# Unused tiles of 32 to 192 bytes between the tiles of a Fourier-mixing and FFN kernel, so that TensorE's weights lie 64 bytes (mod 256) above the operand streamed meanwhile

## The chip, the cores and the metric

The kernel runs on one core of one Trainium2 chip. The metric is the device time of one execution in microseconds (us); the median of several runs is compared. Engines are named as in the profile: PE is TensorE's matmuls, PEld its weight loads, DVE is VectorE, ACT ScalarE, POOL GpSimd, SP the engine that issues most DMAs.

## What is computed

Three layers follow one another on x of shape (4, 3072, 256), all float32:

```
X  = rfft(x, axis=1)                                  # layer 1: Fourier mixing
Yr = soft(Xr @ w_r - Xi @ w_i + b_r)                  # soft(v) = sign(v) * max(|v| - 0.01, 0)
Yi = soft(Xr @ w_i + Xi @ w_r + b_i)
x  = irfft(Yr + i Yi, n=3072, axis=1)
xk = mu_k * x + (1 - mu_k) * x_prev                   # layer 2: FFN with a token shift, 256 -> 1024 -> 256
xr = mu_r * x + (1 - mu_r) * x_prev
x  = sigmoid(xr @ w_r2) * ((max(xk @ w_k, 0) ** 2) @ w_v)
h  = x @ w_in                                         # layer 3: FFN 256 -> 2048 -> 256
out = (h * clip(h + 3, 0, 6) / 6) @ w_out
```

## The kernel before, in words

Each float32 operand is split in two halves, a rounded high part and a low rest, and each product is made of three matmuls: high by high, low by high, high by low (`three`, whose matmul is L156, and `m` inside `u_s`, L698). Every matmul has a weight load of its own: the left operand (the weights, up to 128 x 128) is loaded, then the right operand (192, 256 or 512 columns) is streamed past it. The load for the next matmul is issued while the current one streams. The order of PE, ACT, DVE and POOL is the order in the program (a manual schedule); only SP's queue is placed by the framework.

The work has three stretches. In the first (0 to about 800 us of the span) the Fourier layer of four batches is woven with the first FFN. `s1` (transform along 96), `s2` (transform along 32), `mix` (the complex weights), `ia` and `ib` (the inverse transforms) make the Fourier layer; `u_r`, `u_k` and `u_v` make the first FFN. While `mid` runs, one step holds 24 matmuls of mix, 6 of ia, 12 of s2 and 24 of 512 columns of the FFN. In the second (about 800 to 1105 us) the rest of the first FFN runs while DVE and ACT decode the float64 weights `wi` and `wo` of the second, and the first tile of the second FFN starts (`u_i`). In the third (about 1105 us to the end) 23 tiles of 512 tokens times 8 units, 184 units, are worked off: `u_s` (L682) makes 21 matmuls of a unit with seven products in place of eight, `u_o` (L755) the 24 that sum into the output; they are issued as 12 of u_s, 8 of u_o, 6 of u_s, 8 of u_o, 3 of u_s, 8 of u_o. All 45 stream 256 columns.

Memory: a tile pool lays its tiles one after another in SBUF, in the order in which their tags are first asked for. `cst`, `kb` and `kw` (later `sp` in the place of `kw`) stand one upon another from below, `fp` (later `w2` and `w3`) hangs from the top, so that its first tile moves down when it grows. fp takes 96,768 bytes of a partition, and 3,008 bytes lie free between kw and fp. All tiles that TensorE reads are multiples of 256 bytes in size or cut at such multiples, f1 and fi (384 bytes to each half) excepted; so the address modulo 256 is the same for all buffers of a tag and for all slices that are used.

The functions that the change touches: `stage1` (first buffers of `kb`), `load_chunks` (tag a), `load_t` (tag t), `mix` (tag y), and the body, where the pools' constants and weights are made.

Of the kernel before, what the change touches and what calls it, by code (L numbers as in the profile page):

```python
# [9 lines left out]
F32 = mybir.dt.float32  # L10
# [13 lines left out]
TOK = 512  # L24
# [79 lines left out]
def fourier_mix_ffn_kernel(  # L104
# [32 lines left out]
    cst = ctx.enter_context(tc.tile_pool(name="cst", bufs=1))  # L137
    kb = ctx.enter_context(tc.tile_pool(name="kb", bufs=1))
    kw = ctx.enter_context(ExitStack())
    kw_p = kw.enter_context(tc.tile_pool(name="kw", bufs=1))  # L140

    def ptile(name):
        return ps.tile([128, 1024], F32, tag="h", name=name)

# [5 lines left out]
    def three(o, pairs, first=True, last=True, **kw):  # L150

        n = 3 * len(pairs)
        i = 0
        for (lh, ll), (rh, rl) in pairs:
            for a, c in ((lh, rh), (ll, rh), (lh, rl)):
                nc.tensor.matmul(o, a, c, start=first and i == 0, stop=last and i == n - 1, **kw)  # L156
                i += 1
# [54 lines left out]
    def decoder(jobs, stage):  # L212

        running = []
        for n in range(2 * len(jobs) + 4):
# [5 lines left out]
                running.append(w.decode(w.load(stage, *job), *job))  # L221
            yield

    def stage1():
        w = kb.tile([128, 1024], U32, tag="gh", bufs=3, name="stw")
        return w, kb.tile([128, 2, TOK], F32, tag="gl", bufs=3, name="stt")

    with tc.manual_schedule(engines=order):
        ff = ctx.enter_context(ExitStack())
        fp = ff.enter_context(tc.tile_pool(name="fp", bufs=1, side="right"))  # L230

        f1 = cst.tile([N1, 2, N1], F32R, name="f1")
        fi = cst.tile([N1, 2, N1], F32R, name="fi")
        zero = cst.tile([128, 2, 1], F32, name="zero")
        mus = cst.tile([128, 2, 2], F32, name="mus")
        omu = cst.tile([128, 2, 2], F32, name="omu")
        half = cst.tile([128, 1], F32, name="half")
        top = cst.tile([128, 2, 1], F32, name="top")
        bias = fp.tile([128, 3, D], F32, name="bias")
        tex = fp.tile([128, 2, 64], F32R, name="tex")  # L240

# [5 lines left out]
        head = {"load": 0, "split": 0, "use": 0}  # L247
        live = {}

        def load_chunks(upto):  # L250
            while head["load"] < min(len(chunks), upto) and chunks[head["load"]][1] in ready:
                n = head["load"]
                src, _, p = chunks[n]
                a = fp.tile([128, 2, D], F32, tag="a", bufs=5, name="a")
                nc.sync.dma_start(out=a[:p], in_=src)
                live[n] = (a[:p], p)
                head["load"] += 1
# [45 lines left out]
        def load_t(b, j):  # L303

            if j >= NP + 2:
                b, j = b + 1, j - NP - 2
            if b < B:
                t = fp.tile([128, 2, 640], F32R, tag="t", bufs=3, name="tt")
                c = slice(0 if j < NP else 384, 640 if j >= 2 else 384)
                nc.gpsimd.dma_start(out=t[:, :, c], in_=tab[j, :, :, c])  # L310
                tt[b, j] = t

        def mid(b):
            gb = sc_b[b].rearrange("(j g c) n d -> j (c n) g d", g=2, c=4)
            xx, yy = {}, {}


            at = lambda j, g, dt: (512 * g + (192 if g else 256) * dt) if j == 0 else 384 * g + 192 * dt

            def s2(j):  # L320
                ((h, l),) = take(1)
                t = tt[b, j]
                p = ptile("s2")
                for g in range(2):
                    for dt in range(2):
                        d = slice(128 * dt, 128 * dt + 128)
                        hl = (h[:, g, d], l[:, g, d])
                        if j or g:
                            c = 512 * g + 192 * dt
                            three(p[:, c : c + 192], [(hl, (t[:, g, 0:192], t[:, g, 192:384]))])  # L330
                        else:
                            c = 256 * dt
                            three(p[:, c : c + 64], [(hl, (t[:, g, 0:64], t[:, g, 192:256]))])
                            three(p[:, c + 64 : c + 128], [(hl, (tex[:, 0], tex[:, 1]))])
                            three(p[:, c + 128 : c + 256], [(hl, (t[:, g, 64:192], t[:, g, 256:384]))])
                xh = fp.tile([128, 896], F32R, tag="Xh", bufs=2, name="Xh")
                xl = fp.tile([128, 896], F32R, tag="Xl", bufs=2, name="Xl")
                if j == 0:
                    split(p[:, 0:896], xh, xl)
                else:  # L340
                    two = lambda v: v.rearrange("p (g f) -> p g f", g=2)
                    split(two(p)[:, :, 0:384], two(xh[:, 0:768]), two(xl[:, 0:768]))
                xx[j] = (xh, xl)

            def mix(j):
                xh, xl = xx.pop(j)
                p = ptile("mix")
                for g in range(2):
                    pairs = []
                    for dt in range(2):  # L350
                        c = at(j, g, dt)
                        for c, w in ((c + (64 if j or g else 128), aw[0]), (c, aw[1])):
                            c = slice(c, c + 128)
                            pairs.append(((xh[:, c], xl[:, c]), (w.hi[:, dt], w.lo[:, dt])))
                    three(p[:, 256 * g : 256 * g + 256], pairs)
                y = fp.tile([128, 512], F32, tag="y", bufs=2, name="yf")
                m = fp.tile([128, 512], F32, tag="co", bufs=2, name="ym")
                yh = fp.tile([128, 512], F32R, tag="yh", bufs=2, name="yh")
                yl = fp.tile([128, 512], F32R, tag="yl", bufs=2, name="yl")
                bs = bias[:, 0:2] if j == 0 else bias[:, 1:3]  # L360
                nc.vector.tensor_add(y, p[:, 0:512], bs.rearrange("p g d -> p (g d)"))
                nc.vector.tensor_scalar(m, y, LAM, 0.0, op0=ALU.add, op1=ALU.min)
                nc.vector.scalar_tensor_tensor(y, y, LAM, m, op0=ALU.subtract, op1=ALU.max)
                yy[j] = (y, yh, yl)

            def split_y(j):
                y, *yy[j] = yy[j]
                split(y, *yy[j])

            def ia(j):  # L370
                yh, yl = yy.pop(j)
                t = tt.pop((b, j + 2))[:, :, 384:640]
                p = ptile("ia")
                for g in range(2):
                    c = slice(256 * g, 256 * g + 256)
                    three(p[:, c], [((t[:, g, 0:128], t[:, g, 128:256]), (yh[:, c], yl[:, c]))])
                sb = fp.tile([128, 4, D], F32, tag="ev", bufs=3, name="iasb")
                nc.scalar.activation(sb[:, 0:2].rearrange("p g d -> p (g d)"), p[:, 0:512], AF.Copy)
                nc.sync.dma_start(out=gb[j], in_=sb[:, 0:2])

            for j in range(NP + 1):
                if j < NP:
                    s2(j)
                load_t(b, j + 2)
                if j >= 2:
                    split_y(j - 2)
                if j < NP:
                    yield
                if j:
                    mix(j - 1)  # L390
                    fetch()
                    yield
                if 2 <= j < NP:
                    ia(j - 2)

            def end(j):
                if j + 1 < NP:
                    split_y(j + 1)
                else:
                    load_t(b, NP + 3)  # L400
                    ready.add(("b", b))
                ia(j)

            ends.extend([lambda: end(NP - 2), lambda: end(NP - 1)])
# [53 lines left out]
            later.append(plan("ib", b, 0, 8))  # L458

        aw = [Weights(fp, w, 2, D, f"aw{i}") for i, w in enumerate((w_r, w_i))]  # L460
        wr = Weights(kw_p, w_rr, 2, D, "wr")
        wk = Weights(kw_p, w_k, 2, FF1, "wk")
        wv = Weights(kw_p, w_v, 8, D, "wv")

        nc.gpsimd.dma_start(out=f1.rearrange("p s n -> p (s n)"), in_=small[:, 0 : 2 * N1])
# [348 lines left out]
        for step, _ in enumerate(stream(first)):  # L814
# [4 lines left out]
            if step in SPLIT_MIX:  # L819
                w, staged, job = plain.pop(0)  # L820
# [101 lines left out]
        for n, (i, j) in enumerate(units):  # L922
            if i == 0:
# [9 lines left out]
                if j == 3:  # L933
                    decode_to(len(wi.jobs + wo.jobs) * 2 + 4)
                    stage.close()
                    sp = ctx.enter_context(tc.tile_pool(name="sp", bufs=1))
                    sw = [sp.tile([128, 4, 8, 128], F32R, name=f"sw{c}") for c in range(2)]
                    c0, c1, c2, c3 = (sums(sp, c) for c in range(4))
                    x1 = split_s(sp, 1)
                    beside = {3: c0[:2], 4: c0[2:] + c1[:1], 5: c1[1:], 6: x1[:2], 7: x1[2:] + c2[:1]}  # L940
                    aside = c2[1:] + c3
# [44 lines left out]
```

## Time and profile before

| what | value |
|---|---|
| median of 3 runs | 2080.52 us (2079.47 to 2082.42) |
| profiled execution: its own time | 2082.47 us |
| its span, first to last instruction | 2080.7 us |
| mean granted TensorE clock, share of full speed | 0.976 |
| PE busy, matmuls | 96%, 13,928 |
| DVE, ACT, POOL busy | 74%, 64%, 2% |
| HBM read and written | 110.35 MB, 63.31 MB |

Durations of single matmuls in the profile overlap, since matmuls are pipelined; what one costs is read from the distance of one start to the next. The granted clock of 1.00 is TensorE's level of 2.4 GHz.

### The profile page before, as it was taken

How to read it: one execution, taken by the hardware profiler on the slowest of the kernel's cores; microseconds unless marked ns; L12 is line 12 of the kernel's file. 1: busy time of each engine (PE TensorE's matmuls, PEld its weight loads, DVE VectorE, ACT ScalarE, POOL GpSimd, SP SyncE). 2: the span in 40 equal slices, each digit the busy share in tenths (PEclk: the TensorE clock that was granted, in tenths of full speed). 3: DMA queues.
4: the chain of work that ended last, by engine and by line, in shares of the span. 5: the costliest groups of instructions: out<-in, count | busy, mean ns of one | idle time of the engine just before them, and what ended most of it. 6: DMA issues, size and time to landing. Idle time of an engine off the chain costs nothing.

```text
span 2080.7 us, 33798 instructions
## 1 busy us (share of the span) xinstructions
PE 1992.8 (96%) x13928; PEld 1844.5 (89%) x13928; DVE 1549.8 (74%) x1975; ACT 1323.2 (64%) x1917; POOL 35.0 (2%) x63
## 2 busy tenths in 40 slices
PE   6878999999999999889998999999999999999998
PEld 4867998898789888667787999999999999999998
DVE  3868667777677686767777777877787778777875
ACT  5556447555754565555646777777777777667775
POOL 0000000000000000000000000000000000000000
PEclk7978999999999999999999999999999999999999
DMA  9765447543653352122100001100110011001100
GB/s 265 240 205 165 123 114 228 163 142 115 216 170 111 95 179 65 63 75 77 51 31 24 29 23 29 32 21 23 30 32 21 22 31 32 21 22 31 32 11 21
DMA packets 106988, 175.85 MB, mean 85 GB/s; under 512 B 12945, under 2 KB 63314, under 8 KB 106834
## 3 DMA queue, kind: packets, MB, share of 16 engines
q1 hardware_dynamic: 96034, 141.76, 22.1%
q0 software_dynamic: 10480, 31.67, 5.7%
q8 instruction: 109, 1.79, 0.4%
q14 instruction: 45, 0.37, 0.1%
q10 hardware_dynamic: 320, 0.26, 0.0%
HBM read 110.35 MB, written 63.31 MB: 83 GB/s over the span
## 4 chain that ended last, share of the span: by engine, by line
PE 76%; DVE 14%; ACT 6%; issue 2%; DMA 2%; SPq 0%; ACTq 0%; DVEq 0%
PE oacc L776 24%; PE rq L776 15%; PE acc L156 8%; PE pk L156 7%; PE cc L776 6%; PE mix L156 5%; PE s L156 4%; DVE g L552 2%; DVE gl L553 2%; PE pr L156 2%; DVE xf L511 1%; PE ia L156 1%; DVE kl L518 1%; PE ib L421 1%; PE ib L420 1%
## 5 line engine op out<-in xcount | busy, mean ns | idle before, releaser
L776 PE MATMUL oacc<-wo_hi,gl 128*128 128x256 f32 x1536 | 426.7, 278 | 0.6 <-DVE gl L750 0.6
L776 PE MATMUL oacc<-wo_hi,gh 128*128 128x256 f32 x1536 | 427.1, 278 | 0.0
L776 PE MATMUL oacc<-wo_lo,gh 128*128 128x256 f32 x1536 | 425.4, 277 | 0.0
L776 PEld LDWEIGHTS oacc<-wo_hi,gl 128*128 128x128 f32 x1536 | 288.7, 188 | 1.0 <-DVE gl L750 0.8
L776 PEld LDWEIGHTS oacc<-wo_hi,gh 128*128 128x128 f32 x1536 | 288.5, 188 | 0.2
L776 PEld LDWEIGHTS oacc<-wo_lo,gh 128*128 128x128 f32 x1536 | 288.7, 188 | 0.0
L732 DVE TENSOR_TENSOR c<-rq,s 128x512 f32<-128x512 f32 x184 | 127.3, 692 | 184.2 <-ACT s L728 184.2
L745 DVE SCALAR_TENSOR_TENSOR g<-g,c 128x1024 f32<-128x1024 f32 x184 | 225.5, 1226 | 27.1 <-ACT g L744 17.4
L749 ACT ACTIVATE gh<-g 128x1024 fp32r<-128x1024 f32 x184 | 195.2, 1061 | 55.8 <-DVE g L745 55.8
L750 DVE TENSOR_TENSOR gl<-g,gh 128x1024 fp32r<-128x1024 f32 x184 | 223.7, 1216 | 1.2 <-ACT gh L749 1.2
L776 PE MATMUL rq<-th,sw 128*128 128x256 f32 x1104 | 217.4, 277 | 7.3 <-DVE g L606 7.3
L744 ACT ACTIVATE g<-c,half 128x1024 f32<-128x1024 f32 x184 | 211.5, 1150 | 4.1 <-DVE c L733 1.4
L712 ACT ACTIVATE s<-rq 128x512 f32<-128x512 f32 x184 | 109.9, 598 | 112.0 <-PE rq L776 111.5
L776 PEld LDWEIGHTS rq<-th,sw 128*128 128x128 f32 x1104 | 166.4, 188 | 7.5 <-DVE g L606 7.5
L156 PE MATMUL acc<-gl,wv_hi 128*128 128x512 f32 x384 | 153.8, 400 | 13.3 <-DVE gl L553 13.3
L547 ACT ACTIVATE g<-pk 128x1024 f32<-128x1024 f32 x96 | 97.6, 1016 | 106.5 <-PE pk L156 106.4
L156 PE MATMUL pk<-kh,wk_hi 128*128 128x512 f32 x384 | 152.8, 398 | 9.3 <-ACT kh L517 5.2
L776 PE MATMUL rq<-tl,sw 128*128 128x256 f32 x552 | 153.9, 279 | 2.8 <-DVE tl L679 2.8
L148 DVE TENSOR_TENSOR al<-a,ah 96x512 fp32r<-96x512 f32 (+1 forms) x176 | 114.9, 684 | 55.2 <-ACT ah L147 55.2
L156 PE MATMUL acc<-gh,wv_hi 128*128 128x512 f32 x384 | 153.2, 399 | 1.6 <-ACT gh L551 1.5
L156 PE MATMUL acc<-gh,wv_lo 128*128 128x512 f32 x384 | 152.2, 396 | 0.0
L156 PE MATMUL pk<-kl,wk_hi 128*128 128x512 f32 x384 | 151.9, 396 | 0.0
(150 smaller groups left out, 4953.0 us busy)
## 6 DMA issues: line engine op xcount, KB each, us to landing
tt<-in_tab_dram POOLq DMA_DIRECT2D x40, 640.0 KB, 4.9
yt<-sc_y SPq DMA_DIRECT2D x23, 608.0 KB, 3.9
a<-in_x_dram SPq DMA_DIRECT2D x64, 192.0 KB, 3.5
sc_a<-s1sb SPq DMA_DIRECT2D x32, 384.0 KB, 3.9
a<-sc_a SPq DMA_DIRECT2D x48, 256.0 KB, 3.2
sc_b<-iasb SPq DMA_DIRECT2D x48, 256.0 KB, 4.8
a<-sc_b SPq DMA_DIRECT2D x64, 192.0 KB, 3.1
sc_y<-ysb SPq DMA_DIRECT2D x32, 384.0 KB, 2.9
```

The lines of the kernel that those rows point to most:

```text
L148: nc.vector.tensor_sub(l, src, h.bitcast(F32))
L156: nc.tensor.matmul(o, a, c, start=first and i == 0, stop=last and i == n - 1, **kw)
L547: nc.scalar.activation(g, p, AF.Relu)
L552: nc.vector.tensor_mul(g, g, g)
L553: nc.vector.tensor_sub(l, g, h.bitcast(F32))
L712: nc.scalar.activation(s[:, 1:3].rearrange("p a n -> p (a n)"), rq, AF.Copy)
L732: nc.vector.tensor_add(c[:, 1::2], two(rq), s[:, 0:2])
L744: nc.scalar.activation(g, c, AF.Relu, bias=half, scale=1.0 / 6.0)
L745: nc.vector.scalar_tensor_tensor(g, g, 1.0, c, op0=ALU.min, op1=ALU.mult)
L749: lambda: nc.scalar.activation(h, g, AF.Copy),
L750: lambda: nc.vector.tensor_sub(l, g, h.bitcast(F32)),
L776: return lambda: nc.tensor.matmul(o, lhs, rhs, start=start, stop=stop, skip_group_check=True)
```

## The change

It adds a helper `pad` that takes an unused tile of so many bytes per partition out of a pool, and calls it at 11 places (the arrays `pad_a`, `pad_t`, `pad_y` and `padded` make those in functions happen once). No instruction reads or writes these tiles. Nothing else differs.

```diff
--- before.py
+++ after.py
@@ -139,6 +139,13 @@
     kw = ctx.enter_context(ExitStack())
     kw_p = kw.enter_context(tc.tile_pool(name="kw", bufs=1))
 
+    pads = []
+
+    def pad(pool, n):
+
+        pads.append(n)
+        pool.tile([128, n // 4], F32, name=f"pad{len(pads)}")
+
     def ptile(name):
         return ps.tile([128, 1024], F32, tag="h", name=name)
 
@@ -221,21 +228,29 @@
                 running.append(w.decode(w.load(stage, *job), *job))
             yield
 
+    padded = []
+
     def stage1():
         w = kb.tile([128, 1024], U32, tag="gh", bufs=3, name="stw")
-        return w, kb.tile([128, 2, TOK], F32, tag="gl", bufs=3, name="stt")
+        t = kb.tile([128, 2, TOK], F32, tag="gl", bufs=3, name="stt")
+        if not padded:
+            padded.append(pad(kb, 128))
+        return w, t
 
     with tc.manual_schedule(engines=order):
         ff = ctx.enter_context(ExitStack())
         fp = ff.enter_context(tc.tile_pool(name="fp", bufs=1, side="right"))
 
+        pad(cst, 32)
         f1 = cst.tile([N1, 2, N1], F32R, name="f1")
+        pad(cst, 128)
         fi = cst.tile([N1, 2, N1], F32R, name="fi")
         zero = cst.tile([128, 2, 1], F32, name="zero")
         mus = cst.tile([128, 2, 2], F32, name="mus")
         omu = cst.tile([128, 2, 2], F32, name="omu")
         half = cst.tile([128, 1], F32, name="half")
         top = cst.tile([128, 2, 1], F32, name="top")
+        pad(cst, 96)
         bias = fp.tile([128, 3, D], F32, name="bias")
         tex = fp.tile([128, 2, 64], F32R, name="tex")
 
@@ -247,10 +262,14 @@
         head = {"load": 0, "split": 0, "use": 0}
         live = {}
 
+        pad_a, pad_t, pad_y = [128], [192], [192]
+
         def load_chunks(upto):
             while head["load"] < min(len(chunks), upto) and chunks[head["load"]][1] in ready:
                 n = head["load"]
                 src, _, p = chunks[n]
+                if pad_a:
+                    pad(fp, pad_a.pop())
                 a = fp.tile([128, 2, D], F32, tag="a", bufs=5, name="a")
                 nc.sync.dma_start(out=a[:p], in_=src)
                 live[n] = (a[:p], p)
@@ -305,6 +324,8 @@
             if j >= NP + 2:
                 b, j = b + 1, j - NP - 2
             if b < B:
+                if pad_t:
+                    pad(fp, pad_t.pop())
                 t = fp.tile([128, 2, 640], F32R, tag="t", bufs=3, name="tt")
                 c = slice(0 if j < NP else 384, 640 if j >= 2 else 384)
                 nc.gpsimd.dma_start(out=t[:, :, c], in_=tab[j, :, :, c])
@@ -353,6 +374,8 @@
                             c = slice(c, c + 128)
                             pairs.append(((xh[:, c], xl[:, c]), (w.hi[:, dt], w.lo[:, dt])))
                     three(p[:, 256 * g : 256 * g + 256], pairs)
+                if pad_y:
+                    pad(fp, pad_y.pop())
                 y = fp.tile([128, 512], F32, tag="y", bufs=2, name="yf")
                 m = fp.tile([128, 512], F32, tag="co", bufs=2, name="ym")
                 yh = fp.tile([128, 512], F32R, tag="yh", bufs=2, name="yh")
@@ -458,8 +481,10 @@
             later.append(plan("ib", b, 0, 8))
 
         aw = [Weights(fp, w, 2, D, f"aw{i}") for i, w in enumerate((w_r, w_i))]
+        pad(kw_p, 64)
         wr = Weights(kw_p, w_rr, 2, D, "wr")
         wk = Weights(kw_p, w_k, 2, FF1, "wk")
+        pad(kw_p, 128)
         wv = Weights(kw_p, w_v, 8, D, "wv")
 
         nc.gpsimd.dma_start(out=f1.rearrange("p s n -> p (s n)"), in_=small[:, 0 : 2 * N1])
@@ -934,7 +959,9 @@
                     decode_to(len(wi.jobs + wo.jobs) * 2 + 4)
                     stage.close()
                     sp = ctx.enter_context(tc.tile_pool(name="sp", bufs=1))
+                    pad(sp, 64)
                     sw = [sp.tile([128, 4, 8, 128], F32R, name=f"sw{c}") for c in range(2)]
+                    pad(sp, 192)
                     c0, c1, c2, c3 = (sums(sp, c) for c in range(4))
                     x1 = split_s(sp, 1)
                     beside = {3: c0[:2], 4: c0[2:] + c1[:1], 5: c1[1:], 6: x1[:2], 7: x1[2:] + c2[:1]}
```

The addresses that follow, modulo 256, for the operands of every product: before as the built program lists them, after with the added sizes summed up by hand. The last columns are the distance (weights minus streamed operand, modulo 256).

| product | weights: before, after | streamed: before, after | distance before | distance after |
|---|---|---|---|---|
| s1 | f1 128 / 0, 160 / 32 (high / low) | ah, al 224, 96 | 160 / 32 | 64 / 192 |
| s2 | ah, al 224, 96 | tt 224, 32 | 0 | 64 |
| mix | Xh, Xl 224, 32 | aw 224, 224 | 0 | 64 |
| ia | tt 224, 32 | yh, yl 224, 224 | 0 | 64 |
| ib | ah, al 224, 96 | fi 128, 32 | 96 | 64 |
| u_r, u_k | wr, wk 32, 224 | kh, kl 32, 160 | 0 | 64 |
| u_v | wv 32, 96 | gh, gl 32, 32 | 0 | 64 |
| u_i | wi 224, 224 | xh, xl 32, 160 | 192 | 64 |
| u_s with wi | wi 224, 224 | xh, xl, th, tl 32, 160 | 192 | 64 |
| u_s with sw | sw 32, 224 | th, tl, xh, xl 32, 160 | 0 | 64 |
| u_o | gh, gl 32, 32 | wo 224, 224 | 64 | 64 |

Where one product follows another, the first weights of the second are loaded while the last operand of the first streams: from u_s to u_o the distance is 0 before and 128 after, from u_o to u_s 64 before and 0 after.

## Rows read from the trace of the kernel before

**Rows 1.** The page: busy time of each engine, and the granted TensorE clock in 40 slices.

```profile
PE 1992.8 (96%) x13928; PEld 1844.5 (89%) x13928; DVE 1549.8 (74%) x1975; ACT 1323.2 (64%) x1917; POOL 35.0 (2%) x63
...
PEclk7978999999999999999999999999999999999999
```

**Rows 2.** The page's chain that ended last: by engine; then the chain view by line.

```profile
PE 76%; DVE 14%; ACT 6%; issue 2%; DMA 2%; SPq 0%; ACTq 0%; DVEq 0%
by line: PE oacc L776 24.4%; PE rq L776 15.5%; PE acc L156 7.9%; PE pk L156 7.4%; PE cc L776 6.2%; PE mix L156 5.1%; PE s L156 4.2%; DVE g L552 2.3%; issue 2.0%; DVE gl L553 1.9%; PE pr L156 1.7%; DVE xf L511 1.4%; PE ia L156 1.2%; DVE kl L
```

**Rows 3.** Windows of five stretches; columns: us, busy us (xinstructions) of PE, PEld, DVE, ACT, POOL, PEclk, DMA share, GB/s.

```profile
200.00:312.00 112.00, 112.00 (x710) 101.28 (x710) 78.85 (x103) 54.78 (x76) 5.38 (x10) 1.00 0.42 122
400.00:511.00 111.00, 111.00 (x705) 100.50 (x704) 82.73 (x109) 58.23 (x82) 5.37 (x10) 1.00 0.41 121
600.00:712.00 112.00, 112.00 (x707) 101.19 (x706) 77.09 (x99) 53.09 (x72) 5.36 (x10) 1.00 0.37 107
800.00:1040.00 240.00, 218.60 (x922) 173.88 (x921) 182.45 (x224) 140.06 (x170) 0.00 (x0) 0.98 0.21 69
1119.34:2055.72 936.38, 936.38 (x8075) 936.38 (x8074) 733.28 (x880) 669.66 (x1010) 0.00 (x0) 1.00 0.09 26
```

**Rows 4.** The chain by line within 800 to 1040 us.

```profile
by line: DVE g L552 16.2%; DVE gl L553 15.0%; DVE xf L511 7.8%; DVE kl L518 7.2%; issue 5.3%; ACT gh L551 4.7%; ACT g L547 4.6%; ACT stt L197 4.3%; PE pk L156 4.0%; DVE stt L200 3.6%; PE acc L156 3.4%; ACT stt L198 3.3%; DVE stt L202 3.2%; 
```

**Rows 5.** Timeline of PE's weight loads, 1504 us; columns: start us, us, engine, line, op.

```profile
1504.11 0.19 PEld L776 LDWEIGHTS oacc<-wo_hi,gh 128*128 128x128 f32 x1
```

**Rows 6.** Timeline of PE's matmuls, one unit of the second FFN, 1502.82 to 1508.04 us.

```profile
1502.82 0.39 PE L776 MATMUL rq<-th,sw 128*128 128x256 f32 x2
...
1504.11 0.28 PE L776 MATMUL cc<-tl,wi_hi 128*128 128x256 f32 x1
1504.23 0.28 PE L776 MATMUL oacc<-wo_hi,gh 128*128 128x256 f32 x1
...
1505.15 0.39 PE L776 MATMUL rq<-th,sw 128*128 128x256 f32 x2
...
1505.85 0.28 PE L776 MATMUL oacc<-wo_lo,gh 128*128 128x256 f32 x1
...
1506.77 0.39 PE L776 MATMUL rq<-th,sw 128*128 128x256 f32 x2
...
1507.12 0.28 PE L776 MATMUL oacc<-wo_hi,gl 128*128 128x256 f32 x1
...
1508.04 0.39 PE L776 MATMUL rq<-th,sw 128*128 128x256 f32 x2
```

**Rows 7.** Timeline of PE, 2065.78 to 2072.02 us: first and last of 56 matmuls of u_o.

```profile
2065.78 0.28 PE L776 MATMUL oacc<-wo_lo,gh 128*128 128x256 f32 x1
...
2072.02 0.28 PE L776 MATMUL oacc<-wo_hi,gh 128*128 128x256 f32 x1
```

**Rows 8.** The chain in order of time, one step of the mid stage; start us, us, what.

```profile
221.72 2.87 PE mix L156 x24
224.59 2.76 PE pk L156 x12
227.36 0.71 PE ia L156 x6
228.07 1.32 PE s L156 x12
```

**Rows 9.** Timeline of PE, 240.36 to 242.40 us: nine 512-column matmuls, then mix.

```profile
240.36 0.39 PE L156 MATMUL pk<-kh,wk_hi 128*128 128x512 f32 x1
...
242.40 0.28 PE L156 MATMUL mix<-aw_hi,Xh 128*128 128x256 f32 x1
```

**Rows 10.** Timeline of PE, 327.82 to 328.29 us: a matmul of s1, then acc.

```profile
327.82 0.39 PE L156 MATMUL s<-al,f 96*96 96x512 f32 x1
328.05 0.40 PE L156 MATMUL acc<-gh,wv_hi 128*128 128x512 f32 x1
328.29 0.40 PE L156 MATMUL acc<-gh,wv_lo 128*128 128x512 f32 x1
```

## The prediction

> **What bounds the kernel now.** I read the page first: PE is busy for 96% of the span, and from the fifth of 40 slices on its clock is granted at nine tenths or more [rows 1]. Busy is not the same as bound, so the chain that ended last comes next: 76% of it is PE, DVE 14%; by line the second FFN (oacc, rq, cc) has 46.1%, the 512-column matmuls of the first FFN (acc, pk, pr) 17.0%, mix 5.1% [rows 2]. The windows show where. From 1119 to 2056 us PE never stops, at a granted clock of 1.00, and three windows of the mid stage (112 + 111 + 112 = 335 us) are like it. From 800 to 1040 us PE is busy for 218.6 of 240 us only [rows 3], and the chain there lies on DVE and ACT [rows 4]. So a faster matmul pays one for one in the third stretch and in the mid stage, and next to nothing from 800 to 1040 us.
>
> What one matmul takes is the distance from start to start. At the 2.4 GHz of a granted 1.00, 256 columns would stream in 106.7 ns and 512 in 213.3 ns. The weights of the next matmul are loaded while the present one streams: the load for the first oacc starts at 1504.11 us, with the matmul before it [rows 5, 6]. Against that floor I set four settled runs and the distance (next weights minus streamed operand, mod 256) from the address table:
> - u_o, distance 64: 55 steps in 6.24 us, 113.4 ns each [rows 7], 6.7 over the floor.
> - u_s, distance 192 and 0: 12 in 1.41 us, 117.5 ns [rows 6], 10.8 over.
> - mix, distance 0: 24 in 2.87 us, 119.6 ns [rows 8], 12.9 over; ia, distance 0, 6 in 0.71 us, 118.3 ns.
> - pk, distance 0, 512 columns: 9 in 2.04 us, 226.7 ns [rows 9], 13.4 over.
>
> Two things are to be seen. Three of these have the same shape, engine and clock, and differ by 6 ns; the fastest is the one whose distance is 64 already. And the excess at distance 0 is about the same for 256 and 512 columns, so it belongs to the weight load that comes with each matmul, not to the columns.
>
> **The change part by part.** The pads add no instruction, no wait and no DMA, so no queue (PE's, SP's and POOL's among them) gets anything; their cost is nothing as long as the pools fit and reuse the same predecessors' memory. fp's 96,768 bytes grow by 512, the pools below by 640 with sp's own; the gap between kw and fp was 3,008 bytes. What moves is the distance.
>
> *Second FFN.* A unit takes 5.22 us, 1502.82 to 1508.04 [rows 6], and 936.38 us over 8,075 matmuls gives 116.0 ns, 45 of them 5.22 us again [rows 3]. After the change the 21 matmuls of u_s have distance 64 as u_o's have. With all 45 at 113.4 ns the unit takes 5.103 us. The six places in it where u_s and u_o meet have distances 128 and 0. No row has 128. A price for such an edge: below nothing; above what a u_o stretch pays today for coming after u_s, 8 in 0.92 us against 8 x 0.1134 = 0.907, so 13 ns [rows 6, 7]. I take 9, nearer to the upper end, since three of the six have distance 0, which costs mix 6 ns and is followed by some settling. So 5.103 + 6 x 0.009 = 5.157 us, 63 ns less, and over 184 units **-11.6 us** (-21.5 with free edges, -7.2 at 13 ns).
>
> *Mid stage.* A step is 24 of mix, 6 of ia, 12 of s2 and 24 of 512 columns: 2.87 + 0.71 + 1.32 + 2 x 2.76 = 10.42 us [rows 8], so 335 us are 32 steps. mix gains 24 x 6.2 ns = 0.15 us, ia 6 x 4.9 = 0.03. s2 streams 192 columns in 110 ns, far above the 80 ns that these need, so something else paces it, by its length the weight load: I take no change, bounds minus and plus 3 ns a matmul (-1.2 and +1.2 us in all). The FFN's 512 columns have no settled row at distance 64. Below: the saving of mix, 6.2 ns per weight load. Above: the one place where 512 columns stream at distance 64 now, the last s1 matmul before acc, takes 0.23 us like its neighbours [rows 10], so nothing. I take 6.2 ns, since that single matmul has no settled neighbour and the excess of pk equals that of mix: 24 x 6.2 = 0.15 us. Five new edges at 9 ns give 0.045 back. Sum -0.29 us a step, **-9.3 us** in 32 steps, 4.8 of it from the 512 columns.
>
> *The rest.* The chain holds 17.0% of 2080.7 us, 354 us, of acc, pk and pr [rows 2]; the mid stage has 32 x 5.5 = 176 of them, 178 us are left, 780 matmuls: **-4.8 us** (0 if 512 columns gain nothing). s1 and u_i, of 512 columns too, go from 32, 160 and 192 to 64, one s1 matmul in three to 192: some 200 on the chain at 7 ns, **-1.5 us** (0 to -2). ib goes from 96 to 64 and is paced like s2: nothing. What falls to 800 to 1040 us is lost in DVE's and ACT's waits.
>
> Sum: -11.6 - 9.3 - 4.8 - 1.5 = -27.2 us. From the profiled execution's own 2082.47 us that makes 2055.3; it lies 1.95 us above the median of the runs shown, 2080.52, so the median becomes **2053.5 us**. In the third stretch DVE is busy for 733 of 936 us [rows 3], so it does not take the bound from PE at 1.2% less.
>
> **The rivals.**
> - *Only 256 columns gain* (0.24). For it: the 0.23 us of rows 10; a longer stream could also find its collision later in the row. Against: equal excess for both lengths. It takes away 4.8 + 4.8 + 1.5 us: 2064.5.
> - *The edges are free* (0.06). The 13 ns of today's edges may belong to the conflicting stretch before them. Then -21.5 in place of -11.6 and 1.4 more in the mid stage: about 2042.
> - *Nothing happens* (0.08). The two streams may not meet at all, and the 6 ns come from what differs otherwise between u_o and mix (tiles far apart, tile lengths, neighbours in PSUM). Then 2080.5. The Trainium skill, in TensorE: Matmul & The Clock Gate, section "Step-by-step: what each phase is for", speaks for this: the streamed operand and the weight load have each a read port of SBUF, and loading the next weights takes no bandwidth from the running matmul. By that rule the distance has no effect, 2080.5 us; rows 6 to 8 do not agree, with 113.4 and 119.6 ns for one shape at one clock.
> - *Slower* (0.04). If u_o's 113.4 ns have another cause than the distance, u_s, mix and pk keep their times, while u_o, which stands right today, gets three edges of distance 128 and three of 0 in each unit. At half the settling price for four more disturbed loads, 27 ns a unit, 184 units lose 5 us: 2085.5. It decides if the stretches gain under 27 / 21 = 1.3 ns a matmul.
>
> The forecast itself has 0.56; 0.02 is left for a mishap that takes back most of what is won, such as a new wait where sp meets other predecessors; half of it I count as faster, half as within 0.2%.
>
> **How the numbers follow.** The low end is free edges, the whole gain of 512 columns and s2's bound: 2042. The high end is the first rival with edges at 13 ns: 7.2 us from the third stretch and 4 us from mix and ia, 2069. The forecast and the first rival lie inside, and half of the second: 0.83, of which some of the bounds' own corners are cut off. Faster by over 0.2% (below 2076.4 us, about what a measurement of this kernel can tell from no change) is 0.56 + 0.24 + 0.06 + 0.01 = 0.87; within 0.2%, 0.08 + 0.01 = 0.09; slower 0.04.
>
> **What would show it.** In the changed kernel's trace: 12 matmuls of u_s in 1.36 us in place of 1.41; mix x24 in 2.72 in place of 2.87; settled pk at 220 ns in place of 227 (the step that I am least sure of); u_o unchanged at 113.4 but for its first and last matmuls; the same counts of instructions; 800 to 1105 us of the same length. The forecast is wrong if u_s stays at 117.5 ns, if a unit's edges cost over 20 ns each, or if PE starts to wait in the third stretch.

## The result and the profile after

The changed kernel takes 2095.51 us (median of 6 runs, 2094.92 to 2097.82), the kernel before, run beside it, 2081.45 us (2079.47 to 2083.15). The ratio is 1.0069, 95% interval 1.0056 to 1.0082: **slower by 0.7%**, where 2053.5 us and a gain of 1.3% had been forecast, and outside the range of 2042 to 2069 us. The profiled execution shown here took 2096.12 us, 13.65 us more than that of before; its span is 2094.3 us.

First the page of the changed kernel: busy time, share of the span and instructions, and the clock.

```profile
PE 2008.8 (96%) x13928; PEld 1851.1 (88%) x13928; DVE 1548.9 (74%) x1975; ACT 1322.7 (63%) x1917; POOL 34.9 (2%) x63
...
PEclk7978999999999999999999999999999999999999
```

The counts of instructions and the clock are those of before, and the shares are within one point [rows 1]: no work came in, and PE's own time grew. The windows say where (us, then busy time of PE, PEld, DVE, ACT, POOL with instructions, granted clock, DMA share, GB/s):

```profile
200.00:312.00 112.00, 112.00 (x713) 100.29 (x712) 79.17 (x103) 55.24 (x76) 5.48 (x10) 1.00 0.42 122
...
800.00:1040.00 240.00, 223.13 (x919) 174.33 (x918) 180.32 (x223) 139.23 (x169) 0.00 (x0) 0.97 0.22 69
1119.34:2055.72 936.38, 936.38 (x7953) 936.38 (x7952) 723.03 (x870) 659.62 (x997) 0.00 (x0) 1.00 0.09 26
```

Read the matmul counts against [rows 3]. In the third stretch the same 936.38 us hold 7,953 matmuls, not 8,075: 117.7 ns each in place of 116.0, with PE never idle and a granted clock of 1.00. A unit of 45 takes 5.30 us in place of 5.22, and 184 units x 0.08 us are 14.7 us, more than the whole loss. In the mid stage 112 us hold 713 matmuls in place of 710: slightly faster. From 800 to 1040 us nothing gains, as foreseen.

The timeline of PE in one unit of the changed kernel (start, us, operation, count), the first row of each run of u_s and u_o:

```profile
1533.99 0.40 PE L801 MATMUL rq<-th,sw 128*128 128x256 f32 x2
...
1535.41 0.28 PE L801 MATMUL oacc<-wo_hi,gh 128*128 128x256 f32 x1
...
1536.35 0.40 PE L801 MATMUL rq<-th,sw 128*128 128x256 f32 x2
...
1537.06 0.28 PE L801 MATMUL oacc<-wo_lo,gh 128*128 128x256 f32 x1
...
1538.00 0.40 PE L801 MATMUL rq<-th,sw 128*128 128x256 f32 x2
...
1538.36 0.28 PE L801 MATMUL oacc<-wo_hi,gl 128*128 128x256 f32 x1
...
1539.30 0.28 PE L801 MATMUL rq<-th,sw 128*128 128x256 f32 x1
```

Twelve matmuls of u_s take 1.42 us (118 ns) though their distance is now 64; forecast were 1.36. Each eight of u_o take 0.94 us, 0.92 before [rows 6]. So u_s did not become like u_o; u_o became like u_s.

The chain of a step of the mid stage of the changed kernel (start, us, what):

```profile
219.38 2.82 PE acc L163 x12
222.20 2.74 PE mix L163 x24
224.94 2.79 PE pk L163 x12
227.73 0.69 PE ia L163 x6
228.42 1.32 PE s L163 x12
```

Against [rows 8], mix fell from 2.87 to 2.74 (forecast 2.72), ia by 0.02 (0.03), s2 stayed; but 12 of 512 columns rose from 2.76 to 2.79 and 2.82 (233 to 235 ns), where 220 ns had been forecast. The step takes 10.36 us, 0.06 less.

### The profile page after: what moved, and what is told of

Read it like the earlier page. It is cut to its first block, busy times and chain, and to the rows that moved or that the text cites. A ratio compares the mean times of both kernels' runs of the same rounds, so it can differ in the third digit from the quotient of the medians.

```text
span 2094.3 us, 33798 instructions
## 1 busy us (share of the span) xinstructions
PE 2008.8 (96%) x13928; PEld 1851.1 (88%) x13928; DVE 1548.9 (74%) x1975; ACT 1322.7 (63%) x1917; POOL 34.9 (2%) x63
## 4 chain that ended last, share of the span: by engine, by line
PE 76%; DVE 13%; ACT 6%; DMA 2%; issue 2%; SPq 0%; ACTq 0%; DVEq 0%
PE oacc L801 25%; PE rq L801 16%; PE acc L163 8%; PE pk L163 7%; PE cc L801 6%; PE mix L163 5%; PE s L163 4%; DVE g L577 2%; DVE gl L578 2%; PE pr L163 2%; DVE xf L536 1%; PE ia L163 1%; DVE kl L543 1%; PE ib L444 1%; PE ib L443 1%
## 5 line engine op out<-in xcount | busy, mean ns | idle before, releaser
L801 PE MATMUL oacc<-wo_hi,gl 128*128 128x256 f32 x1536 | 432.0, 281 | 0.5 <-DVE gl L775 0.5
L801 PE MATMUL oacc<-wo_lo,gh 128*128 128x256 f32 x1536 | 430.7, 280 | 0.0
L801 PEld LDWEIGHTS oacc<-wo_hi,gh 128*128 128x128 f32 x1536 | 293.5, 191 | 0.2
L801 PE MATMUL rq<-th,sw 128*128 128x256 f32 x1104 | 222.4, 284 | 7.7 <-DVE g L631 7.7
L769 ACT ACTIVATE g<-c,half 128x1024 f32<-128x1024 f32 x184 | 210.7, 1145 | 2.2 <-DVE c L758 1.4
L163 PE MATMUL pk<-kh,wk_lo 128*128 128x512 f32 x384 | 153.0, 398 | 0.0
```

Of the source, the lines that this page charges most:

```text
L769: nc.scalar.activation(g, c, AF.Relu, bias=half, scale=1.0 / 6.0)
L801: return lambda: nc.tensor.matmul(o, lhs, rhs, start=start, stop=stop, skip_group_check=True)
```

## The experiments

The theory after the result: the distance does set the pace, but 64 is no cure by itself; what comes before matters, so that one set of addresses can run at one of two lasting paces, called rhythms below (theory R), and 512 columns answer differently. Rivals: the price lies in the edges alone (E), or in other engines that work beside PE (O).

**m1_map: bare matmuls on PE.** Only matmuls on two tiles, the weights and the streamed operand shifted by multiples of 32 bytes; no other engine works beside them.

```diff
+        run(512, 0, 48)
+        for n in (256, 512):
+            for entry in (0, 64, 128, 192):
+                for d in range(0, 256, 32):
+                    run(n, entry, 8)
+                    run(n, d, 24)
...
+        for _ in range(12):
+            unit(0, 0, 192, 0, 192)
+        for _ in range(12):
+            unit(0, 128, 192, 192, 192)
```

> Nothing but matmuls on PE, weights and streamed operand in two tiles at chosen addresses; no Fourier layer and no FFN is computed. Stretches of 24 at distances 0, 32, ... 224 (mod 256), 256 and 512 columns, each entered from 8 matmuls at 0, 64, 128 or 192; then the unit of 45 matmuls of the second FFN twelve times with the distances of before and twelve times with those of the change. Theory R (two lasting rhythms): distance 64 with 256 columns settles at 113.4 ns after some entries and stays at about 118 ns after others, for all 24; 512 columns at 64 take 233 ns, at 0 227 ns; the units come out as in the two traces, 5.22 and 5.30 us. Rival E (edges alone): every stretch at 64 falls back to 113.4 ns after at most 4 matmuls, whatever it is entered from. Rival O (other engines): with DVE, ACT and DMA silent, 64 is 113.4 ns throughout, 512 columns gain too (220 ns), and the changed unit is shorter than the old one, 5.16 us.

Windows of m1_map (us, PE, PEld, ACT, POOL, clock, DMA share, GB/s). The first pair is 256 columns at distance 64, entered from eight matmuls at 0 and at 64; the second is 512 columns at 64 and at 0:

```profile
29.40:32.11 2.71, 2.71 (x25) 2.71 (x24) 0.00 (x0) 0.00 (x0) 1.00 0.00 0
59.58:62.19 2.61, 2.61 (x25) 2.61 (x24) 0.00 (x0) 0.00 (x0) 1.00 0.00 0
158.10:163.47 5.37, 5.37 (x24) 4.33 (x23) 0.00 (x0) 0.00 (x0) 1.00 0.00 0
143.42:148.64 5.22, 5.22 (x24) 4.32 (x23) 0.00 (x0) 0.00 (x0) 1.00 0.02 3
```

The first two windows are each 23 steps from start to start: 117.8 and 113.3 ns by the starts themselves (the windows are rounded to 10 ns), one shape at one distance and one clock, and each pace lasts through all 24. The two others are 23 steps of 233.4 and 226.8 ns. Settled ns per matmul, worked out from the starts of the last 13 of each 24:

| distance | 256 columns | 512 columns |
|---|---|---|
| 0 | 120.0 | 226.7 |
| 64 | 113.3 (entered from 64, 128) or 117.8 (from 0, 192) | 233.3 |
| 192 | 113.3 (from 0, 64) or 117.8 (from 128, 192) | 228.8 |
| all others | 116.7 to 120.0 | 231.7 to 234.2 |

Four stretches with the streamed operand 32 bytes further on show that the distance run before is not all that counts: there 64 took 113.5 ns straight after 24 matmuls at 0, where the table has 117.8. 192 columns take 111.5 to 111.8 ns at every distance, which fits s2, which did not move. The last part runs twelve units with the distances of before, then twelve with those of the change (a window counts every matmul that reaches into it):

```profile
411.72:474.38 62.66, 62.66 (x543) 62.66 (x541) 0.00 (x0) 0.00 (x0) 1.00 0.00 1
474.38:537.86 63.48, 63.48 (x541) 63.48 (x540) 0.00 (x0) 0.00 (x0) 1.00 0.00 1
```

Twelve of the first take 62.66 us, 5.22 each. The second window is one matmul short of twelve units: (63.48 + 0.118) / 12 = 5.30. Both kernels' units, to 10 ns, with every other engine silent: for these two sets of distances O falls, and matmuls alone give the loss (for the set of v1_all192, below, bare units and the full kernel differ). E falls too, since the whole of a run is slow and not its ends. The rule of the Trainium skill that the prediction weighed (TensorE: Matmul & The Clock Gate, "Step-by-step: what each phase is for"), by which the load of the next weights takes no bandwidth from the running matmul, does not agree with 120.0 and 113.3 ns here, where only addresses differ.

**r2_fourier, r3_second, r4_first: the change in three parts.** Each keeps some of the pads and drops the others.

```diff
 r2_fourier, against the changed kernel
-            padded.append(pad(kb, 128))
...
-        pad(kw_p, 64)
...
-        pad(kw_p, 128)
...
-                    pad(sp, 64)
...
-                    pad(sp, 192)
 r3_second: the pads of kb, sp and the 128 of kw stay, all others go
 r4_first: only pad(kw_p, 64) stays
```

> The change with its pads in cst and fp alone: s1, s2, mix, ia and ib have the new distances, the first FFN stays at 0, the second FFN as before. Theory R: mix 24 in about 2.78 us in place of 2.87, 512 columns 227 ns, unit 5.22 us: some 6 us faster than before, 2075. Rival O: mix keeps its 2.78 us too, but the other engines' new addresses disturb the rest: no gain or a loss, 2081 or more.

> The pads of kb and sp (and the one before wv, which keeps the first FFN at distance 0) alone: u_s goes to 64, the edges to 128 and 0, u_i to 64, all else as before. Theory R and rival E: the unit takes 5.30 us in place of 5.22, 184 units give +14.7 us, 2096. If the loss lies in the first FFN's 512 columns in place of that, the unit stays under 5.24 us and the time under 2085.

> One pad of 64 bytes ahead of wr alone: the first FFN's 512-column matmuls go from distance 0 to 64, all else as before. Theory R: 233 ns in place of 227 to 229, some 1,550 of them on the chain: +6 to +9 us, 2088 to 2091. Rival O: 220 ns in the mid stage, a gain of up to 9 us.

| kernel | us | ratio, interval | unit | mid step |
|---|---|---|---|---|
| r2_fourier | 2077.24 | 0.9975 [0.9965, 0.9984] | 5.22 | 10.34 |
| r3_second | 2097.95 | 1.0071 [1.0054, 1.0088] | 5.30 | 10.42 |
| r4_first | 2085.08 | 1.0012 [1.0002, 1.0021] | 5.22 | 10.51 |

The kernel before took 2083.23 us beside them. The windows of r3_second and of r2_fourier for the same stretch, one kernel each:

```profile
1130.00:1330.00 200.00, 200.00 (x1700) 200.00 (x1700) 155.66 (x187) 140.75 (x213) 0.00 (x0) 1.00 0.09 25
```

```profile
1130.00:1330.00 200.00, 200.00 (x1726) 200.00 (x1726) 157.46 (x190) 143.51 (x217) 0.00 (x0) 1.00 0.09 26
```

1,700 matmuls are 37.7 units of 5.30 us, 1,726 are 38.3 of 5.22. So the loss sits in the pads of the second FFN, the gain in those of the Fourier layer, and the first FFN's pad costs a little. -0.25% + 0.71% + 0.12% = +0.58%, against +0.69% for the whole, within the intervals. In r4_first the mid step shows the first FFN's price:

```profile
221.34 2.86 PE mix L163 x24
224.20 2.80 PE pk L163 x12
...
229.04 2.81 PE pk L163 x12
```

2.80 and 2.81 us are 0.04 to 0.05 above 2.76 [rows 8]; at 0.09 us a step, 32 steps lose 2.9 us. The whole kernel lost 1.85 us, where 6 to 9 had been expected. Where DVE and ACT set the pace, the slower matmuls cost nothing, as the window of r4_first from 800 to 1040 us shows:

```profile
800.00:1040.00 240.00, 223.53 (x924) 174.20 (x923) 182.15 (x224) 140.17 (x170) 0.00 (x0) 0.98 0.21 68
```

PE was busy for 223.53 us in place of 218.60 and still came to 924 matmuls, 922 before [rows 3]. r2_fourier gained less than expected too, 2077.24 us for 2075. It has its 512 columns at distance 0, and its chain shows mix in the slow rhythm, 2.83 us where 2.78 had been expected, though its distance is 64:

```profile
221.43 2.83 PE mix L163 x24
224.26 2.72 PE pk L163 x12
```

That is 117.9 ns, not the 114 of the changed kernel, where mix follows 512 columns at 64. So part of mix's gain there came with the distance of its neighbour.

**m2_units: bare units with 72 sets of addresses**, and a test of whose weights count.

```diff
+        for n in (256, 512):
+            for k in range(48):
+                mm(n, 64 * ((k + 1) % 2), 64 * (k % 2))
+            for k in range(48):
+                mm(n, 64 * (k % 2), 64 * (k % 2))
+        for g in (64, 192):
+            for x0 in (0, 64, 128, 192):
+                for dw in (0, 64, 192):
+                    for ds in (0, 64, 192):
+                        for _ in range(4):
+                            unit(g, x0, (x0 + dw) % 256, (x0 + ds) % 256, 0)
```

> Nothing but matmuls on PE again. First two stretches of 48 for 256 and for 512 columns, with the streamed operand at two places 64 bytes apart in turn: in the first the next weights lie at distance 0 from the operand streamed, in the second each matmul's own weights do (the next ones then at 64 and 192 in turn). If the distance that counts is that of the next weights, the first takes 120 and 227 ns a matmul and the second 113 to 118 and 229 to 234; if it is that of a matmul's own weights, the other way round. Then the unit of 45 in 72 sets of addresses, four units each: distance of u_o 64 or 192, of u_s with wi and with sw 0, 64 or 192 each, and four places of the operand streamed in u_s relative to that of u_o, which set the distances at the edges. Theory R (entry decides the rhythm): the set of before gives 5.22 us and that of the change 5.30 as in m1_map; sets that share the distances inside the stretches and differ only at the edges differ by up to 45 x 4.5 ns = 0.2 us; the best comes near 45 x 113.4 ns = 5.10 us. Rival E (each edge has a price, the stretches settle by their own distance): sets with the same distances inside lie within six edges of 13 ns, 0.08 us, of one another, and all with 64 inside below 5.18 us.

Windows of the two stretches of 256 columns, 47 steps each, first with the next weights at distance 0 and the own ones at 64 and 192 in turn, then the other way round (columns as for m1_map):

```profile
20.72:26.36 5.64, 5.64 (x49) 5.64 (x47) 0.00 (x0) 0.00 (x0) 1.00 0.01 3
26.48:31.97 5.49, 5.49 (x50) 5.49 (x48) 0.00 (x0) 0.00 (x0) 1.00 0.00 0
```

They are 120.0 and 116.8 ns a matmul on the mean, as expected if the next weights count. For 512 columns, 233.3 and 231.8, neither near 227: undecided. The 72 sets give units from 5.10 to 5.34 us. With 192 inside all stretches, the four places of u_s's streamed operand give 5.10 to 5.30, where rival E allowed 0.08 us. Windows of m2_units, two units each (columns as for m1_map): all distances 64 with the edges too; the same with sw at 192; the set of before; that of the change:

```profile
144.50:155.10 10.60, 10.60 (x92) 10.60 (x91) 0.00 (x0) 0.00 (x0) 1.00 0.00 0
165.52:175.72 10.20, 10.20 (x93) 10.20 (x92) 0.00 (x0) 0.00 (x0) 1.00 0.01 2
373.80:384.24 10.44, 10.44 (x93) 10.44 (x92) 0.00 (x0) 0.00 (x0) 1.00 0.01 2
710.18:720.78 10.60, 10.60 (x92) 10.60 (x91) 0.00 (x0) 0.00 (x0) 1.00 0.00 0
```

Halved: 5.30, 5.10, 5.22 and 5.30 us. Even 64 at every matmul, edges included, gave 5.30 here. With the streamed operands of u_s and u_o at the same address (mod 256) and distances of 64 and 192 alone, seven of eight sets give 5.10, which is the 45 x 113.4 ns of the prediction.

**v1_all192, v2_all64, v3_64_192: three layouts for the kernel itself.** All keep the Fourier pads, put the first FFN's 512 columns back to distance 0, and give the streamed operands of u_s and u_o one address (mod 256), so that edges have the same distances as runs. They differ in the distances of the second FFN: 192 everywhere; 64 everywhere; 64, but 192 where the weights are sw.

```diff
 v3_64_192, against the changed kernel
-            padded.append(pad(kb, 128))
+            padded.append(pad(kb, 192))
...
-        pad(kw_p, 64)
...
-        pad(kw_p, 128)
+        pad(kw_p, 64)
         wv = Weights(kw_p, w_v, 8, D, "wv")
...
+                    pad(w2, 192)
...
-                    pad(sp, 64)
+                    pad(sp, 192)
                     sw = [sp.tile([128, 4, 8, 128], F32R, name=f"sw{c}") for c in range(2)]
-                    pad(sp, 192)
+                    pad(sp, 64)
 v2_all64: as v3_64_192, but sp keeps 64 ahead of sw and 192 behind
 v1_all192: kb 128 ahead of the first tile and 64 behind, kw 192, w2 64, sp as in v3_64_192
```

> The Fourier pads of the change as in r2_fourier, the first FFN back at distance 0, and in the second FFN every distance, inside the stretches and at the edges, at 192. By the units of m2_units, which gave 5.100 us for this set from the first unit on: 184 units x 0.120 us = 22 us less than r2_fourier, about 2055 us, ratio to before near 0.987. If other engines' traffic matters on the chip's full kernel, the unit is longer than 5.10 us.

> As v1_all192, but every distance of the second FFN at 64, edges too; inside the stretches this is what the change has, and only the edges differ from it (64 in place of 128 and 0). Theory R: nothing in this unit moves the rhythm from one to the other, so a unit takes 5.10 or 5.30 us, whichever rhythm it was entered with, and little between; m2_units entered it slow and stayed at 5.300 for all four units. 2055 or 2092 us, more likely the second, or a mixture if a wait resets the rhythm. Rival E (edges have a price and no memory): with no edge that differs, 5.10 us and 2055.

> As v2_all64, but u_s with sw at 192, so 64 and 192 take turns within the unit. By m2_units 5.100 us, reached within one unit from a slow one: 2055 us, ratio near 0.987. If it is the mere presence of distance 64 inside u_o that costs, 5.2 us or more, 2074.

| kernel | us | ratio, interval |
|---|---|---|
| v1_all192 | 2095.59 | 1.0069 [1.0054, 1.0084] |
| v2_all64 | 2091.53 | 1.0046 [1.0029, 1.0063] |
| v3_64_192 | **2065.88** | **0.9925 [0.9910, 0.9940]** |

The kernel before took 2081.36 us beside them. v1_all192 is a miss: its units are 5.30 us from the first to the last. A window of it:

```profile
1130.00:1330.00 200.00, 200.00 (x1700) 200.00 (x1700) 155.74 (x187) 139.99 (x212) 0.00 (x0) 1.00 0.09 25
```

In m2_units the same distances gave 5.10, but there they followed units of 5.10 us; a slow start was not tried. Distance 192 has a slow rhythm too, 117.8 ns in m1_map, and 45 of those are 5.30 us. That the kernel entered it slow is likely and not shown; other engines' traffic is not ruled out here.

v2_all64 is the most telling. Its windows, each 61.20 us long: the first ahead of a stall at 1219.85 us, the second behind it, the third far behind:

```profile
1151.28:1212.48 61.20, 61.20 (x542) 61.20 (x541) 47.82 (x57) 44.65 (x68) 0.00 (x0) 1.00 0.10 27
1228.17:1289.37 61.20, 61.20 (x522) 61.20 (x521) 46.09 (x55) 43.22 (x66) 0.00 (x0) 1.00 0.10 25
1800.00:1861.20 61.20, 61.20 (x522) 61.20 (x521) 49.35 (x61) 43.59 (x67) 0.00 (x0) 1.00 0.10 27
```

Same addresses, same instructions: 542 matmuls, twelve units of 5.10 us, and then 522, units of 5.30, to the end. What lies between is in the timeline of v2_all64, PE first and then ACT:

```profile
1219.73 0.28 PE L800 MATMUL oacc<-wo_hi,gl 128*128 128x256 f32 x1
1219.85 0.48 PE L800 MATMUL rq<-th,sw 128*128 128x256 f32 x2
1220.16 0.28 PE L800 MATMUL rq<-tl,sw 128*128 128x256 f32 x1
```

```profile
1219.19 0.58 ACT L736 ACTIVATE s<-rq 128x512 f32<-128x512 f32 x1
```

The two rq matmuls take 0.48 us together, 0.40 elsewhere, and the next starts 0.31 us after the first in place of 0.23: a stall of 0.08 us. ACT's copy of s out of rq had ended at 1219.77, just ahead of it; that the late copy causes the stall is read from the trace, and no run took it away. From there each of 162 units is 0.20 us longer, 32 us from 0.08. But not every stall does this. The same run had a longer one before, waiting for DVE's `tl`; first the timeline of PE, then the view of waits from 1145 to 1152 us (us in total, times, longest):

```profile
1145.76 0.39 PE L800 MATMUL rq<-th,sw 128*128 128x256 f32 x2
1146.28 0.38 PE L800 MATMUL rq<-tl,sw 128*128 128x256 f32 x1
```

```profile
PEld rq L800 <- DVE tl L703: 0.3, 1, 0.3
```

The third matmul starts 0.52 us after the first in place of 0.23, and yet the twelve units of 5.10 us of the first window come after it. What tells the two stalls apart is not shown.

v3_64_192 beats both kernels. In its third stretch 923.66 us hold 8,103 matmuls, 114.0 ns each:

```profile
1119.34:2043.00 923.66, 923.52 (x8103) 922.48 (x8102) 735.14 (x883) 666.50 (x1013) 0.00 (x0) 1.00 0.10 26
```

It stalls at the same place of the unit, just behind ACT's copy of s out of rq. Its timeline, ACT and PE:

```profile
1261.44 0.59 ACT L736 ACTIVATE s<-rq 128x512 f32<-128x512 f32 x1
```

```profile
1262.08 0.51 PE L800 MATMUL rq<-th,sw 128*128 128x256 f32 x2
```

But after five to eight matmuls at some 118 ns it is back at 113 by itself: six of eight units stay at 5.10 us, two take 5.17 to 5.31, 5.13 on the mean. The expected 2055 us were missed by 11 us. These stalls make 5.5 of them (184 x 0.03), a mid step of 10.37 us in place of r2_fourier's 10.34, with mix in its slow rhythm, 1 more; the rest is not accounted for.

**m3_mid: the mid step, bare, in 128 sets of addresses.**

```diff
+        for aw in (0, 64, 128, 192):
+            for dx in (64, 192):
+                for t in (0, 64, 128, 192):
+                    for dy in (64, 192):
+                        for da in (64, 192):
+                            for a, b in ((0, 0), (64, 0), (64, 0), (64, 0)):
+                                many(256, aw + dx, aw, 24)
+                                many(512, a, a, 12)
+                                many(256, t, t - dy, 6)
+                                many(192, t + da, t, 12)
+                                many(512, b, b, 12)
```

> Nothing but matmuls on PE: the step of the mid stage (24 of mix, 12 of 512 columns, 6 of ia, 12 of 192 columns, 12 of 512 columns) in 128 sets of addresses, four steps each; the 512-column matmuls at distance 0 in two places, as in v3_64_192; mix, ia and s2 at 64 or 192; the places of their streamed operands in four steps of 64 bytes. Theory R: the set of v3_64_192 gives its 10.36 to 10.38 us; others differ by the rhythm that mix is entered in, 24 x 4.5 ns = 0.11 us, and ia with 0.03; the best near 10.22 us. If the edges into the 512-column matmuls matter more than mix's rhythm, the sets that differ only in them spread by more than 0.11 us. Its best set is then to be carried into the kernel.

The steps take 10.32 to 10.42 us, and the layout of v3_64_192 10.36. The 10.22 us expected of the best set were missed: after 512 columns at distance 0, mix stays at 2.83 us at every one of its addresses. Windows of the 24 of mix and of a whole step, in the set of v3_64_192 (columns as for m1_map):

```profile
196.73:199.56 2.83, 2.83 (x26) 2.83 (x24) 0.00 (x0) 0.00 (x0) 1.00 0.00 0
196.73:207.09 10.36, 10.36 (x67) 9.39 (x66) 0.00 (x0) 0.00 (x0) 1.00 0.01 2
```

The best set would give 32 x 0.04 = 1.3 us and was not built into the kernel.

## Why the prediction was wrong

- **"With all 45 at 113.4 ns the unit takes 5.103 us": the step that failed.** It took a settled row [rows 7] for a property of distance 64. It was one of two lasting rhythms at that distance, 113.3 and 117.8 ns (m1_map). 5.10 us do exist (m2_units, v3_64_192), but no run showed them at the change's addresses. The changed unit took 5.30 us, and the term came out at +14.7 us, not -11.6.
- **"I take 9" for an edge.** The form was wrong, not only the size. Edges were priced as a toll that is over after a few matmuls. Sets of m2_units that differ in nothing but their edges lie up to 0.20 us a unit apart: what happens there lasts through what follows. The changed unit has edges of 128 and 0, as foreseen, and stays at 117.7 ns on average. That this costs 80 ns a unit more than before, whose edges are at 0 and 64, no rule from the map gives; the units had to be run whole.
- **"24 x 6.2 = 0.15 us" for the 512 columns: wrong sign; and the -4.8 and -1.5 us for the rest did not come.** They rose to 233 ns; distance 0 is the best for them (226.7). u_i's rose as well, from 2.76 to 2.79 us for 12. So the equal excess of pk and mix did not mean an equal gain, and the single row at distance 64 [rows 10], 0.23 us, which already spoke against 220 ns, was set aside for having no settled neighbour. r4_first puts the price at +0.12%.
- **mix, ia, s2: right in size, mix partly by luck.** 2.74 against 2.72 us, -0.02 against -0.03, no change; the Fourier pads alone gain (r2_fourier), but there mix comes to 2.83 only: it owes two thirds of its gain to the neighbour that lost.
- **What bounds the kernel: right.** PE waits for nothing in the third stretch, the counts stayed, 800 to 1040 us gave nothing.
- **The rivals.** "Slower" had the right sign and place, u_o losing at its edges, with 27 ns a unit for 80 measured, and the wrong condition: it needed the distance to have no effect. "Nothing happens" fell with m1_map. "Only 256 columns gain" was right in that 512 columns do not. "The edges are free" fell with the unit of 5.30 us.

What adds up: +14.7 us in the third stretch, 32 x 0.06 = -1.9 in the mid stage, together +12.8 of the +13.65 us between the profiled executions; the 512 columns outside the mid stage lie in what is left. (The prediction's own sum ends at 2053.3 us, not 2053.5; nothing hangs on it.)

## What to carry to other kernels

A settled time per matmul belongs to its stretch, with its neighbours and entries, not to the one number by which it was sorted; before carrying it over, look for the same number at another pace, and time the whole repeating unit bare. If a layout has a fast and a slow rhythm, ask which of them it returns to after a stall, and which it has from a slow start: v2_all64 and v3_64_192 reach the same 5.10 us, and only the second comes back to it each time. Operands of 512 columns were best left at distance 0 here.

## What was not expected

- Two lasting rhythms with one set of addresses, 113.3 and 117.8 ns at 256 columns: a stall of 0.08 us in v2_all64 cost some 32 us.
- Distances modulo 256 were enough to repeat the units of the two kernels to 10 ns on an otherwise silent core, 5.22 and 5.30 us in m1_map. They were not enough for v1_all192, 5.10 us bare and 5.30 in the kernel.
- What stays open: why there are two rhythms, what decides which one a stretch is entered in or falls into after a stall, and for 512 columns whether the own or the next weights count.
